# Attention plus gated mixer on one core: where the guard's flag is made, where block 1 is transposed, and where three small masks are built

## The chip, the cores and the metric

One Trainium2 chip, one core. The metric is the device time of one launch in microseconds, smaller is better. A core has a matrix engine (PE, with its weight loads as a row of their own, PEld), VectorE (DVE), ScalarE (ACT), GpSimd (POOL) and the sync engine (SP), which mostly issues DMAs. Each engine works through its own instructions in program order and waits on semaphores that others raise.

## The reference

```python
xn = layernorm(x)                               # 2048 tokens, 512 wide
out = x + A(xn, wqkv, wo) + B(xn, w_in, w_sp, b_sp, w_out)

A:  q, k, v = split(xn @ wqkv)                  # 32 heads of 16
    scores = q @ k.T * 16 ** -0.5, masked to 0 <= i - j < 256
    return softmax(scores) @ v @ wo
B:  z = gelu(xn @ w_in)                         # 1376 wide, halves of 688
    z1, z2 = z[:, :688], layernorm(z[:, 688:])
    g = w_sp @ z2 + b_sp[:, None]               # w_sp: 2048 x 2048
    return (z1 * g) @ w_out
```

## The kernel before

The tokens lie in 16 blocks of 128. The kernel has three stages, and in each the program order of every engine is written out by hand.

**Start.** The loads of x and w_in are issued on SP's and ScalarE's queues. Ten matmuls on zeros (`heat`) run meanwhile, and VectorE and POOL build constants: the identity, and the band masks `maskY` and `maskD`. From `maskD` VectorE builds `maskC` with three small instructions (L235, L238, L242); it is first read by `do_mask` in the second stage. Then, for blocks 0 to 3: statistics of x (`ln_sums` L249, `ln_single`: L253 and L267), the reciprocal root as a power on POOL (L270), and `ln_apply` (L290), which writes `xn`. `transposes` turns the four 128x128 chunks of `xn` on PE (L306) and ScalarE copies the result to `xnT` (L309); from block 4 on this is a DMA instead (L299). Block 0 is turned in two parts.

**Stage 1.** For each block z = gelu(xn @ w_in): `z_mm` (L317) adds up four chunks c of the 512 inputs, in two halves of 688 and in two pieces j of 344 for each. For block 0 the first two chunks of both halves are done first (eight matmuls), then block 1 is transposed, then `z_rest(0)` adds chunks 2 and 3 of the first half, and `z_split(1)` does block 1's first half in two separate banks (`zo`); `z_rest(1)` comes behind. Between the z of later blocks come the projections to q, k and v (`qkv_unit`). PE runs in program order, so an instruction that waits holds up all behind it.

**Stage 2.** A text `ORDER` lists the steps: S scores and their exponentials, m masks, p products with v, n normalization, g the token mixing, f the output. `f_work(t, c0)` makes one output block `fo` in a PSUM bank (two banks, tag f, shared with o and gf): 6 matmuls with w_out (L539), 4 with wo (L546); then VectorE adds x to it (L553), which frees the bank, and a DMA writes it out (L557). At the start of each `f_work` the x of block t + 2 is loaded on SP (`load_xo`, L524; four buffers). Block 15 is done in two halves of 256 columns, written out by SP and by ScalarE. ORDER ends with `p p f n n 10 f10 f10 f10 f10`: two products, the start of block 12, the last two normalizations, block 12, 13, 14, and the two halves of 15.

**The guard.** The softmax is computed without subtracting a maximum. `check_sums` tests all reciprocals of the sums (`r_all`) against two limits (L719, L720, which also counts), and moves the 128 counts to one row by a small DMA on SP (L725). `make_flag` takes the row's minimum (L730) and compares it (L733), and `read_flag` loads the flag into a register of every engine (L739). `tc.If` (L928) then runs a safe version of the whole where the flag is set; here it is not, and every engine branches past it. `check_sums` is called at the end of the last `normalize`, `make_flag` ahead of the add of block 15's first half, and `read_flag` ahead of the add of its second. Behind the branch come some semaphore steps and a barrier of all engines (shown as L953), where SP also waits for the last DMAs.

Of the kernel before, what the change touches and what calls it, by code (L numbers as in the profile page):

```python
# [8 lines left out]
P = 128  # L9
# [3 lines left out]
ALU = mybir.AluOpType  # L13
# [9 lines left out]
HALF = 344  # L23
NB = S_TOK // P
NC = D // P
NG = 4
NJ = NB // 2
# [7 lines left out]
PAD = 64  # L35
# [17 lines left out]
def kernel(  # L53
# [12 lines left out]
    nc = tc.nc  # L66
# [16 lines left out]
    maskD = pers.tile([P, P], BF, name="maskD")  # L83
    maskC = pers.tile([P, 2, PAD], BF, name="maskC")
# [8 lines left out]
    flag = pers.tile([P, 1], mybir.dt.int32, name="flag")  # L93
# [48 lines left out]
    with ExitStack() as actx:  # L142
# [50 lines left out]
        for _ in range(WARM):  # L193
# [9 lines left out]
            out=hmask[:],  # L203
            in_=ident[:].rearrange("p (s e d) -> p e s d", s=4, e=2),
# [3 lines left out]
        for m, off, old, new in ((maskY, 0, PAD, 0), (maskD, -PAD, 0, PAD)):  # L208
            nc.gpsimd.memset(m[:], 1.0)
            nc.gpsimd.affine_select(  # L210
                out=m[:, old : old + PAD], in_=m[:, old : old + PAD], pattern=[[-1, PAD]],
# [3 lines left out]
                out=m[:, new : new + PAD], in_=m[:, new : new + PAD], pattern=[[1, PAD]],  # L215
# [12 lines left out]
        def write_ones():  # L228
# [3 lines left out]
                in_=one[p0:p1, :].unsqueeze(1).to_broadcast([p1 - p0, m1 - m0, H]),  # L232
            )

        nc.vector.tensor_tensor(  # L235
            out=maskC[:, 0, :], in0=maskD[:, 0:PAD], in1=maskD[:, PAD:P], op=ALU.add
        )
        nc.vector.tensor_scalar(  # L238
            out=maskC[:, 1, :], in0=maskC[:, 0, :], scalar1=-1.0, scalar2=1.0,
            op0=ALU.mult, op1=ALU.add,  # L240
        )
        nc.vector.tensor_copy(out=maskC[0:PAD, 1, :], in_=maskC[0:PAD, 0, :])  # L242

        mvx = {}
        rsx = {}

# [5 lines left out]
        def ln_mean(n, b0, mvt, stats):  # L252
            nc.vector.bn_aggr(out=mvt[:, n - b0, :], in_=stats[:])  # L253
            mvx[n] = mvt[:, n - b0, 0:1]
# [4 lines left out]
        def ln_single(n, stats):  # L259
            mvt = sm.tile([P, 4, 2], F32, name="mvt")  # L260
            ln_mean(n, n, mvt, stats)
            rsx[n] = rstd(mvt, 1)[:, 0:1]

        def rstd(mvt, k):
            ve = sm.tile([P, 4], F32, name="ve")
            rs = sm.tile([P, 4], F32, name="rs")
            nc.vector.tensor_scalar(  # L267
                out=ve[:, 0:k], in0=mvt[:, 0:k, 1], scalar1=LN_EPS, scalar2=None, op0=ALU.add
            )
            nc.gpsimd.tensor_tensor(  # L270
                out=rs[:, 0:k], in0=ve[:, 0:k], in1=mhalf[:, 0:k], op=ALU.pow
            )
            return rs
# [11 lines left out]
        def ln_apply(n, parts=1):  # L285
            xs = xts[n // 4][:, n % 4, :]
            xn = lt.tile([P, D], BF, name="xn")
            w = D // parts
            for i in range(parts):
                nc.vector.tensor_scalar(  # L290
                    out=xn[:, i * w : (i + 1) * w], in0=xs[:, i * w : (i + 1) * w],
                    scalar1=mvx[n], scalar2=rsx[n], op0=ALU.subtract, op1=ALU.mult,
                )
            return xn

        def transposes(n, xn, parts=1):
            t0 = PAD + n * P
            if n >= 4:
                nc.sync.dma_start_transpose(out=xnT[:, :, t0 : t0 + P], in_=xn[:])  # L299
                return  # L300
            w = NC // parts
            for i in range(parts):
                tp = psum["f"].tile([P, w, P], BF, name="tp", tag="f")
                for c in range(w):
                    k = i * w + c
                    nc.tensor.transpose(  # L306
                        out=tp[:, c, :], in_=xn[:, k * P : (k + 1) * P], identity=ident[:]
                    )
                nc.scalar.copy(out=xnT[:, i * w : (i + 1) * w, t0 : t0 + P], in_=tp[:])  # L309

        def z_tile():
            return ps_s.tile([P, 2, 512], F32, name="zp", tag="S")

        def z_mm(n, half, j, out, chunks):
            f0 = half * FH + j * HALF
            for c in chunks:
                nc.tensor.matmul(  # L317
                    out, lhsT=xnT[:, c, PAD + n * P : PAD + (n + 1) * P],
                    rhs=w_in_sb[:, c, f0 : f0 + HALF],
                    start=(c == 0), stop=(c == NC - 1),  # L320
                )
# [45 lines left out]
        xns = {}  # L367
        ln_single(0, ln_sums(0))
        sums1 = ln_sums(1)
        xns[0] = ln_apply(0, 2)  # L370
        ln_single(1, sums1)
        xns[1] = ln_apply(1)
        ln_single(2, ln_sums(2))
        sums3 = ln_sums(3)
# [2 lines left out]
        xns[3] = ln_apply(3)  # L377
        transposes(0, xns.pop(0), 2)
        zps = [z_tile(), z_tile()]
        for c in range(2):  # L380
            for half in range(2):
                for j in range(2):
                    z_mm(0, half, j, zps[half][:, j, 0:HALF], [c])
        transposes(1, xns.pop(1))

        def z_rest(half):
            for c in range(2, NC):
# [7 lines left out]
        for n in range(NB):  # L395
            b, j = divmod(n, 4)
# [132 lines left out]
    def f_cols(t):  # L529
        return D // 2 if t == NB - 1 else D  # L530

    def f_work(t, c0):
        if c0 == 0 and t + 2 < NB:
            load_xo(t + 2)
        xo = xos[t]
        w = f_cols(t)
        fo = ps_x.tile([P, 512], F32, name="fo", tag="f")
        for ch in range(NFC):
            nc.tensor.matmul(  # L539
                fo[:, 0:w], lhsT=uTs[t][:, ch, :], rhs=w_out_sb[:, ch, c0 : c0 + w],  # L540
                start=(ch == 0), stop=False,
            )
            yield
        q0 = t % 2 * P
        for c in range(NC):
            nc.tensor.matmul(  # L546
                fo[:, 0:w], lhsT=oTs[t // 2][:, c, q0 : q0 + P], rhs=wo_sb[:, c, c0 : c0 + w],
                start=False, stop=(c == NC - 1),
            )
            yield  # L550
        if t == NB - 1:
            (read_flag if c0 else make_flag)()
        nc.vector.tensor_tensor(  # L553
            out=xo[:, c0 : c0 + w], in0=fo[:, 0:w], in1=xo[:, c0 : c0 + w], op=ALU.add
        )
        eng = nc.scalar if c0 else nc.sync
        eng.dma_start(out=out2[t * P : (t + 1) * P, c0 : c0 + w], in_=xo[:, c0 : c0 + w])  # L557

    E = {}
    ED = {}  # L560
    turned = {}
    later = []
# [39 lines left out]
    def normalize(J, G):  # L602
        ot = turned.pop((J, G))
        rsum = r_all[:, J * NG + G, :]
        nc.vector.reciprocal(out=rsum, in_=ot[:, :, DH])
        on = late().tile([P, 8, 32], BF, name="on", bufs=2)
        nc.vector.tensor_tensor(
            out=on[:].rearrange("p b (e d) -> p e b d", e=2),
            in0=ot[:].rearrange("p (e b) j -> p e b j", e=2)[:, :, :, 0:DH],
            in1=rsum.rearrange("p (e b) -> p e b", e=2).unsqueeze(3).to_broadcast([P, 2, 8, DH]),  # L610
            op=ALU.mult,
        )
        if G == 0:
            oTs[J] = late().tile([P, NC, 256], BF, name="oT", bufs=3)
        nc.vector.transpose(
            out=oTs[J][:, G, :], in_=on[:].rearrange("p b j -> p (b j)")
        )
        if (J, G) == (NJ - 1, NG - 1):
            check_sums()

    groups = [(0, 0, "P"), (0, 1, "P"), (0, 0, "Q"), (0, 0, "D")]
    groups += [(0, 2, "P"), (0, 3, "P"), (0, 2, "Q")]
# [86 lines left out]
        mul(cells(G)[:, 8:16, 0:4:2, :], both[:, 0:1, :].to_broadcast([P, 2, PAD]))  # L709

    rows = []
    again = []

    def check_sums():
        assert not (later or units)
        r = r_all[:].rearrange("p a b -> p (a b)")
        ok = ep.tile([P, 512], BF, name="ok", tag="E")
        low = ep.tile([P, 1], F32, name="low", tag="E")
        nc.vector.tensor_scalar(out=ok[:], in0=r, scalar1=R_LOW, scalar2=None, op0=ALU.is_ge)  # L719
        nc.vector.scalar_tensor_tensor(  # L720
            out=ok[:], in0=r, scalar=R_HIGH, in1=ok[:], op0=ALU.is_le, op1=ALU.mult,
            accum_out=low[:],
        )
        row = ep.tile([P, P], F32, name="row", tag="E")
        nc.sync.dma_start(out=row[0:1, :], in_=low[:])  # L725
        rows.append(row)

    def make_flag():
        low = sm.tile([P, 1], F32, name="low")
        nc.vector.tensor_reduce(  # L730
            out=low[0:1, :], in_=rows[0][0:1, :], axis=mybir.AxisListType.X, op=ALU.min
        )
        nc.vector.tensor_scalar(  # L733
            out=flag[0:1, :], in0=low[0:1, :], scalar1=16.0 * NJ * NG, scalar2=None, op0=ALU.is_lt
        )

    def read_flag():
        again.append(
            nc.values_load(  # L739
                flag[0:1, 0:1], min_val=0, max_val=1,  # L740
                skip_runtime_bounds_check_because="a comparison gives 0 or 1",
            )
        )


# [154 lines left out]
    units = [(J, G) for J in range(NJ) for G in range(NG)]  # L900
# [6 lines left out]
    for step in ORDER.split():  # L907
# [8 lines left out]
        else:  # L916
# [7 lines left out]
            if left == 0:  # L924
                assert next(unit, None) is None
    assert not (left or groups or masks or units or later or any(work.values()))
    late_ctx.close()
    with tc.If(again[0] > 0):  # L928
        with ExitStack() as gctx:
            attention_with_maximum(gctx)  # L930

# [26 lines left out]
```

## Time and profile before

| | us |
|---|---|
| median of 3 runs | 258.0 (257.42 to 259.27) |
| profiled execution, time | 257.84 |
| profiled execution, span | 256.0 |
| PE busy | 249.4 (97%) |
| VectorE busy | 203.6 (80%) |
| ScalarE busy | 194.0 (76%) |
| POOL busy | 20.6 (8%) |

Granted PE clock: 1.000. The span runs from the first to the last instruction; the profiled execution's time is 1.8 us longer.

Busy time by stretch (us from the start of the span, number of instructions in brackets):

```profile
0.00:4.00 4.00, 2.73 (x7) 1.04 (x8) 2.70 (x14) 0.03 (x1) 1.85 (x12) 1.00 0.49 169
4.00:8.00 4.00, 3.07 (x22) 1.53 (x20) 2.80 (x10) 2.11 (x4) 1.12 (x2) 1.00 1.05 366
8.00:13.00 5.00, 4.91 (x40) 3.24 (x38) 4.07 (x14) 4.33 (x8) 1.10 (x2) 1.00 1.01 364
13.00:83.00 70.00, 70.00 (x400) 38.56 (x397) 52.46 (x152) 42.42 (x68) 9.95 (x15) 1.00 0.37 72
83.00:242.00 159.00, 159.00 (x3149) 90.36 (x3150) 134.00 (x222) 145.10 (x156) 6.53 (x19) 1.00 0.52 103
242.00:247.00 5.00, 4.88 (x76) 2.59 (x69) 4.81 (x12) 0.00 (x0) 0.00 (x0) 1.00 0.22 43
247.00:252.00 5.00, 4.77 (x32) 2.83 (x29) 2.51 (x7) 0.00 (x0) 0.00 (x0) 1.00 0.47 131
252.00:256.00 4.00, 0.00 (x0) 0.00 (x0) 0.29 (x1) 0.00 (x0) 0.00 (x0) 1.00 0.17 43
```

The columns are the stretch, its length, the busy time of PE, PEld, VectorE, ScalarE and POOL, PE's clock, the DMA engines' busy share and GB/s. Waits are put down to what came last; lines as "L317" are lines of the kernel, and a q behind an engine's name (SPq) is its sequencer or queue.

### The profile page before, as it was taken

What the parts mean: (1) busy time and instruction counts of PE and PEld (TensorE: products, weight loads), DVE (VectorE), ACT (ScalarE), POOL (GpSimd) and SP (SyncE); (2) the same over time, 40 slices, a digit from 0 to 9 for tenths busy, and PEclk for the clock granted to TensorE, in tenths of its full rate; (3) what the DMA queues carried; (4) which work ended last, traced back from release to release, by engine and by line L of the source; (5) the groups of instructions that cost most, each with busy time, mean ns of one, the idle gap of its engine ahead of it and who ended that gap; (6) DMA issues with size and microseconds to landing.
All of it is one profiled execution on the core that took longest, in us unless ns stands there. A gap on an engine that the chain in (4) does not pass through costs nothing.

```text
span 256.0 us, 8488 instructions
## 1 busy us (share of the span) xinstructions
PE 249.4 (97%) x3700; PEld 140.2 (55%) x3700; DVE 203.6 (80%) x426; ACT 194.0 (76%) x234; POOL 20.6 (8%) x50
## 2 busy tenths in 40 slices
PE   6999999999999999999999999999999999999993
PEld 2655555555555465565455655556456554556642
DVE  7798976974747787988887978688797899788872
ACT  2776468466456999989889989988989999999100
POOL 3232111111011240000000000000000000000000
PEclk9999999999999999999999999999999999999999
DMA  6969341028200236883547082729616568270223
GB/s 244 361 150 255 62 63 22 1 60 120 67 1 0 60 50 138 115 141 81 142 35 188 26 197 57 159 62 160 157 43 97 117 108 166 79 130 28 41 68 89
DMA packets 65689, 26.50 MB, mean 103 GB/s; under 512 B 55872, under 2 KB 63856, under 8 KB 65648
## 3 DMA queue, kind: packets, MB, share of 16 engines
q1 hardware_dynamic: 64784, 24.89, 46.5%
q10 hardware_dynamic: 864, 1.03, 1.2%
q8 instruction: 30, 0.49, 0.9%
q14 instruction: 11, 0.09, 0.1%
HBM read 8.41 MB, written 2.10 MB: 41 GB/s over the span
## 4 chain that ended last, share of the span: by engine, by line
PE 94%; DVE 3%; DMA 1%; issue 0%; ACT 0%; POOL 0%; DVEq 0%
PE gf L503 31%; PE zp L317 14%; PE S L634 10%; PE o L592 9%; PE fo L539 8%; PE pj_o L110 6%; PE fo L546 5%; PE pj_f L110 4%; PE pj_f L128 3%; PE pj_o L128 2%; DMA xt<-in_A_x_dram 1%; DVE ot L599 1%; PE zo L317 1%; DVE xo L553 0%; PE tp L306 0%
## 5 line engine op out<-in xcount | busy, mean ns | idle before, releaser
L684 ACT ACTIVATE E<-S 128x1024 bf16<-128x1024 f32 x124 | 116.9, 1045 | 8.9 <-PE S L634 8.7
L503 PE MATMUL gf<-z2n,wspT 128*128 128x344 bf16 x512 | 83.0, 310 | 0.0
L503 PEld LDWEIGHTS <-wspT 128*128 128x128 bf16 x512 | 46.5, 98 | 29.3 <-issue 7.9
L317 PE MATMUL zp<-w_in_sb,xnT 128*128 128x344 bf16 x248 | 40.9, 309 | 0.2 <-ACT xnT L309 0.2
L690 DVE TENSOR_TENSOR E<-E,maskY 128x2048 bf16<-128x2048 bf16 (+1 forms) x34 | 37.6, 1115 | 3.1 <-ACT E L684 3.1
L317 PEld LDWEIGHTS <-xnT 128*128 128x128 bf16 x256 | 24.8, 98 | 16.0 <-ACT xnT L309 0.8
L634 PE MATMUL S<-qpad,kT 32*128 32x256 bf16 (+2 forms) x848 | 31.7, 260 | 0.0
L662 ACT ACTIVATE ED<-S 128x1024 bf16<-128x1024 f32 x30 | 29.3, 1041 | 0.5 <-PE S L634 0.5
L599 DVE STREAM_TRANSPOSE ot<-o 128x512 f32<-128x512 f32 x32 | 22.2, 715 | 7.4 <-PE o L592 7.4
L509 DVE SCALAR_TENSOR_TENSOR u<-gf,b_all,z 128x344 bf16<-128x344 f32 x32 | 18.3, 572 | 8.5 <-PE gf L503 8.1
L539 PE MATMUL fo<-w_out_sb,uT 128*128 128x512 bf16 (+1 forms) x102 | 24.6, 367 | 0.2
L634 PEld LDWEIGHTS <-kT 32*128 32x128 bf16 (+1 forms) x848 | 11.1, 98 | 21.6 <-issue 20.7
L592 PE MATMUL o<-E,v_y 128*32 128x128 bf16 (+1 forms) x736 | 22.8, 239 | 0.0
L121 DVE TENSOR_SCALAR qpad<-qt,hmask 128x512 bf16<-128x512 bf16 x32 | 9.8, 348 | 14.3 <-ACT qt L119 14.3
L592 PE MATMUL o<-ED,vh 128*32 128x64 bf16 x960 | 21.0, 193 | 0.0
L325 ACT ACTIVATE z2n<-zp 128x688 bf16<-128x688 f32 x16 | 11.9, 744 | 10.8 <-PE zp L317 10.7
L110 PE MATMUL pj_o<-xnT,wqkv 128*128 128x512 bf16 x76 | 19.5, 379 | 0.0
L110 PEld LDWEIGHTS <-wqkv 128*128 128x128 bf16 x128 | 12.5, 98 | 12.6
L325 ACT ACTIVATE z<-zp 128x688 bf16<-128x688 f32 x15 | 11.2, 744 | 10.8 <-PE zp L317 10.8
L690 DVE TENSOR_TENSOR ED<-ED,maskC 128x2048 bf16<-128x2048 bf16 x15 | 18.1, 1204 | 0.0
L270 POOL TENSOR_TENSOR rs<-ve,mhalf 128x2 f32<-128x2 f32 (+1 forms) x18 | 12.0, 667 | 67.9 <-DVE ve L267 67.9
L592 PEld LDWEIGHTS <-vh 128*32 128x32 bf16 x960 | 17.2, 98 | 0.1
(73 smaller groups left out, 240.6 us busy)
## 6 DMA issues: line engine op xcount, KB each, us to landing
vh<-v_y SPq DMA_DIRECT2D x16, 140.0 KB, 3.1
xo<-in_A_x_dram SPq DMA_DIRECT2D x16, 128.0 KB, 2.5
out_dram<-xo SPq DMA_DIRECT2D x15, 128.0 KB, 2.4
xt<-in_A_x_dram SPq DMA_DIRECT2D x3, 512.0 KB, 5.3
wqkv<-in_A_wqkv_dram SPq DMA_DIRECT2D x1, 1536.0 KB, 8.7
w_out_sb<-in_B_w_out_dram SPq DMA_DIRECT2D x1, 640.0 KB, 6.0
wo_sb<-in_A_wo_dram SPq DMA_DIRECT2D x1, 512.0 KB, 4.0
w_in_sb<-in_B_w_in_dram ACTq DMA_DIRECT2D x1, 344.0 KB, 4.2
```

Source lines behind the costliest of these rows:

```text
L110: nc.tensor.matmul(pt[:], lhsT=wqkv[:, c, w0 : w0 + P], rhs=xnT[:, c, t0 : t0 + 512], start=(c == 0), stop=(c == NC - 1),)
L317: nc.tensor.matmul(out, lhsT=xnT[:, c, PAD + n * P : PAD + (n + 1) * P], rhs=w_in_sb[:, c, f0 : f0 + HALF], start=(c == 0), stop=(c == NC ...
L325: nc.scalar.activation(out=dst.rearrange("p (j f) -> p j f", j=2), in_=zp[:, :, 0:HALF], func=ACT.Gelu_apprx_tanh,)
L503: nc.tensor.matmul(gf[:, 0:HALF], lhsT=wspT[t][:, c, :], rhs=z2n[:, c, j * HALF : (j + 1) * HALF], start=(c == 0), stop=(c == NB - 1),)
L509: nc.vector.scalar_tensor_tensor(out=u[:, j * HALF : (j + 1) * HALF], in0=gf[:, 0:HALF], scalar=b_all[:, t : t + 1], in1=z1[:, t, j * HALF ...
L539: nc.tensor.matmul(fo[:, 0:w], lhsT=uTs[t][:, ch, :], rhs=w_out_sb[:, ch, c0 : c0 + w], start=(ch == 0), stop=False,)
L592: nc.tensor.matmul(o[32 * s : 32 * s + 32, c0 + r0 : c0 + r0 + n], lhsT=v[:, m, h * VW : h * VW + 32], rhs=rhs(s), start=(i == 0), stop=(i ...
L599: nc.vector.transpose(out=ot[:].rearrange("p b j -> p (b j)"), in_=o[:])
L634: nc.tensor.matmul(out, lhsT=kT[32 * s : 32 * s + 32, g, k0 : k0 + nk], rhs=qpad[J // 2][32 * s : 32 * s + 32, g, :, qs - q00 : qs - q00 + ...
L662: nc.scalar.activation(out=Ed[:, 16 * i : 16 * i + 16, :], in_=S[i][:].rearrange("p b (x q) -> p (b x) q", q=PAD), func=ACT.Exp, scale=SM_ ...
L684: nc.scalar.activation(out=E[(J, G)][:, b0 + 2 * i : b0 + 2 * i + 2, :], in_=S[i][:], func=ACT.Exp, scale=SM_SCALE,)
L690: nc.vector.tensor_tensor(out=v, in0=v, in1=mask.unsqueeze(1).to_broadcast([P, v.shape[1], *mask.shape[1:]]), op=ALU.mult,)
```

## The change

Three parts. The three instructions that build `maskC` move from the constants to behind `ln_single(1, ...)`, ahead of block 1's apply. Block 1's transposes move ahead of the last two of block 0's first eight z matmuls. `check_sums` is called at the end of the first `f_work` that ends with no product and no normalization left (block 12), behind its add and output; `make_flag` and `read_flag` are called behind everything else, right ahead of `tc.If`.

```diff
-        nc.vector.tensor_tensor(
-            out=maskC[:, 0, :], in0=maskD[:, 0:PAD], in1=maskD[:, PAD:P], op=ALU.add
-        )
-        nc.vector.tensor_scalar(
-            out=maskC[:, 1, :], in0=maskC[:, 0, :], scalar1=-1.0, scalar2=1.0,
-            op0=ALU.mult, op1=ALU.add,
-        )
-        nc.vector.tensor_copy(out=maskC[0:PAD, 1, :], in_=maskC[0:PAD, 0, :])
...
         xns[0] = ln_apply(0, 2)
         ln_single(1, sums1)
+        nc.vector.tensor_tensor(
+            out=maskC[:, 0, :], in0=maskD[:, 0:PAD], in1=maskD[:, PAD:P], op=ALU.add
+        )
+        nc.vector.tensor_scalar(
+            out=maskC[:, 1, :], in0=maskC[:, 0, :], scalar1=-1.0, scalar2=1.0,
+            op0=ALU.mult, op1=ALU.add,
+        )
+        nc.vector.tensor_copy(out=maskC[0:PAD, 1, :], in_=maskC[0:PAD, 0, :])
         xns[1] = ln_apply(1)
...
         zps = [z_tile(), z_tile()]
-        for c in range(2):
-            for half in range(2):
-                for j in range(2):
-                    z_mm(0, half, j, zps[half][:, j, 0:HALF], [c])
-        transposes(1, xns.pop(1))
+        for c, half in ((0, 0), (0, 1), (1, 0), (1, 1)):
+            if (c, half) == (1, 1):
+                transposes(1, xns.pop(1))
+            for j in range(2):
+                z_mm(0, half, j, zps[half][:, j, 0:HALF], [c])
...
-        if t == NB - 1:
-            (read_flag if c0 else make_flag)()
         nc.vector.tensor_tensor(
             out=xo[:, c0 : c0 + w], in0=fo[:, 0:w], in1=xo[:, c0 : c0 + w], op=ALU.add
         )
         eng = nc.scalar if c0 else nc.sync
         eng.dma_start(out=out2[t * P : (t + 1) * P, c0 : c0 + w], in_=xo[:, c0 : c0 + w])
+        if not (rows or units or later):
+            check_sums()
...
-        if (J, G) == (NJ - 1, NG - 1):
-            check_sums()
...
     def read_flag():
-        again.append(
-            nc.values_load(
-                flag[0:1, 0:1], min_val=0, max_val=1,
-                skip_runtime_bounds_check_because="a comparison gives 0 or 1",
-            )
+        return nc.values_load(
+            flag[0:1, 0:1], min_val=0, max_val=1,
+            skip_runtime_bounds_check_because="a comparison gives 0 or 1",
         )
...
+    make_flag()
     late_ctx.close()
-    with tc.If(again[0] > 0):
+    with tc.If(read_flag() > 0):
         with ExitStack() as gctx:
             attention_with_maximum(gctx)
```

More of the change, by code (lines that the diff above doesn't have):

```diff
@@ L711 @@
     rows = []
-    again = []
     def check_sums():
```

## The prediction

> **What bounds the kernel now.** I read the page, then the chain of waits in order of time for the first 14 us and from 240 us on, then the timelines there, the rows of single lines, and the DMA rows of the last 4 us. The page gives PE 97% busy and 94% of the chain, at clock 1.00. In the table by stretches PE is busy for all of 13 to 242 us, so a saving can only lie in the first 13 us, in the last 14, or in being carried unchanged through the middle. The end, in the chain of waits:
>
> ```profile
> 245.16 0.45 DVE oT L615
> 245.60 0.32 DVE ok L719
> ...
> 246.65 0.61 DVE xo L553
> ...
> 247.30 1.45 PE fo L539 x6
> ...
> 251.87 0.42 DVE xo L553
> ```
>
> Columns: start, us, what. VectorE's two range checks (L719, L720) stand ahead of the add of block 12 (L553), which frees the PSUM bank for block 14. After 252.29 the page's chain has nothing, though the span runs to 256.0 (256.03 in the trace). The DMA rows of 251.0 to 255.4 us, 40 slices of 0.11 us, show what fills it:
>
> ```profile
> DMA  0004998200000593000069202104100100000000
> GB/s 28 0 0 149 317 372 280 75 0 0 0 0 0 172 433 98 5 0 0 23 195 312 65 0 79 19 9 93 9 9 5 14 19 5 0 0 0 0 0 0
> q8 instruction: 1, 0.02, 1.8%
> q14 instruction: 3, 0.02, 1.7%
> out_dram<-xo SPq DMA_DIRECT2D x1, 64.0 KB, 3.4
> out_dram<-xo ACTq DMA_DIRECT2D x1, 64.0 KB, 2.8
> ```
>
> Block 15's two output halves (issued 251.61 and 252.32) move nearly all their bytes by 252.8 and 253.4, then a trickle goes on to 254.7; they land at 251.61 + 3.4 = 255.0 and 252.32 + 2.8 = 255.1. The same stretch holds four instruction fetches; in the trace's packets they run one after another, 252.64 to 253.94, then 253.37 to 254.40, and the last output packets follow them. So one DMA engine serves the fetches, and the last sixteenth of both halves queues behind. The fetches follow the guard's branches:
>
> ```profile
> L928 PEldq COMPARE_BRANCH x1: 358/358/358, 251.5 to 251.5; - x1
> L928 SPq COMPARE_BRANCH x1: 58/58/58, 252.6 to 252.6; - x1
> L928 SPq EVENT_SEMAPHORE x3: 17/17/17, 253.1 to 253.3; - x3
> L953 SPq EVENT_SEMAPHORE x10: 17/28/28, 253.4 to 256.0; - x10
> ```
>
> PE branches at 251.50 and the first fetch packet starts 1.14 later. SP's closing waits are done by 253.73 but for those on the two landings, the last met at 255.17; 0.87 of barrier follows, to 256.03.
>
> The start, in the timeline:
>
> ```profile
> 6.35 0.56 POOL L270 TENSOR_TENSOR rs<-ve,mhalf 128x1 f32<-128x1 f32 x1 [0.99 <-DVE ve L267]
> 6.54 1.34 PE L317 MATMUL zp<-w_in_sb,xnT 128*128 128x344 bf16 x8 [0.21 <-ACT xnT L309]
> 6.95 0.41 DVE L290 TENSOR_SCALAR xn<-xt,mvt,rs 128x512 bf16<-128x512 bf16 x1 [0.68 <-POOL rs L270]
> 7.72 0.39 PE L306 MATMUL tp<-ident,xn 128*128 128x128 bf16 x4
> 8.14 0.59 ACT L309 COPY xnT<-tp 128x512 bf16<-128x512 bf16 x1 [1.38 <-PE tp L306]
> 8.78 1.34 PE L317 MATMUL zo<-w_in_sb,xnT 128*128 128x344 bf16 x8
> ```
>
> PE issues a z matmul every 0.146 us; block 0's last one starts at 8.38, so zo could start at 8.53. It starts at 8.78, after the copy of block 1's transpose: a hole of 0.26.
>
> **Block 1's transposes ahead of two z matmuls.** They start two matmuls, 0.29 us, earlier: 7.43. Their input (apply at 6.95, 0.41 long, then 0.056 as from the first apply to its transpose) is there at 7.42, 0.01 early. The copy then ends at 8.43, ScalarE being idle, and zo starts at 8.53: minus 0.26. Next late is nothing: block 0's Gelu starts at 8.73 as now (it waits for the matmul ending at 8.69); the loads of w_in's remaining chunks land at 7.99 and 8.81 and are wanted at 9.7; block 2's apply ends at 9.88 and is wanted at 10.3, block 3's at 11.23, wanted at 11.7; wqkv lands at 14.7, wanted at 15.6. Those covers shrink by 0.26 and hold. The middle carries the 0.26, PE having no other wait there; it is worth 0 if one appears, and 0.26 cannot be exceeded. I take 0.26, since every wait that is listed for PE itself lies before 8.8 us.
>
> **The masks.** Three VectorE instructions leave 2.96 to 3.58. That gains nothing: the first statistics start at 3.61, when ScalarE's queue passes a wait on the same load of x, also at 3.61. The load ends there. In the new place VectorE idles 0.68 before the apply at 6.95, waiting for POOL. The rows before give steps of 0.23 and 0.22 between the masks and 0.17 for the third, 0.62 in all; from 6.2 to 6.3 they end at 6.8 to 6.9. Cost 0; without that cover 0.6 on block 1's apply. They now run beside POOL's power (6.35). Powers last 0.55 to 0.74 us; the longest, 0.73 and 0.74, have VectorE's TENSOR_SCALAR beside them, others with it 0.69. So 0 to 0.05, and I take 0.
> [...]
>
> **The end: range check behind block 12's add.** L719 and L720 (0.42 and 0.62 from start to start) leave the place ahead of that add, which moves from 246.56 to about 245.53. PE gets block 14's bank early, but is itself busy until 247.10 (block 13 began at 244.94; six and four matmuls of 0.216). So fo of block 14 starts at 247.10, not 247.30: minus 0.20. On SP the row's DMA, with 3.6 us of waiting, stood ahead of the load of xo 14 (issued 247.38, landed 249.7, with 1.8 us of VectorE idle for it). Now the load stands ahead and can go at 243.1, behind the uT transpose; the output that its buffer held before was issued at 218.6. The add of block 14 follows PE at 249.5 instead of 249.82. The row goes behind block 12's output, at about 247.4 for 0.53; xo 15's load follows at 248.05 instead of 248.54 and, with 2.54 as now, lands at 250.6. Block 15's halves then follow PE: adds near 250.7 and 251.66 (now 251.16 and 251.87). ScalarE issues the last output at 252.12.
>
> **The end: flag and branch last.** The flag is now made behind the last add. Steps as in the trace: reduce 0.34 behind the start of a 0.43 us add (it starts 0.08 before the add of block 14 ends), 252.00; flag 0.30 later, 252.30; loads on all five engines 0.17 later, 252.47; SP's load 0.53 and 0.08, branch at 253.08; 0.53 to the next instruction, 253.61; 0.70 of semaphores, 254.31; 0.87 of barrier, 255.18. Queued behind the loads is only the branch and the barrier, but all engines wait for them. Cover: by the 1.14 above, fetches start near 254.2, when the last output, moved 1.1 to 1.55 us after its issue, has landed at 253.7. So a landing at 255.1 is exchanged for a flag chain that ends at 254.3; the end goes from 256.03 to 255.18, minus 0.85, the 0.20 in it. Bounds: loads took 0.47 to 0.58 and branch to next instruction 0.17 (POOL) to 0.61 (VectorE), so plus or minus 0.2.
>
> **Sum.** 256.03 - 0.26 - 0.85 = 254.92; the profiled execution took 257.84, 1.81 outside its span: 256.73. The median of the three runs is 0.16 higher: 256.9.
>
> **Rivals.** *The fetches still meet the output* (they follow the stream's pages, not the branch). Then the late sixteenth stays, and only 0.20 and 0.26 are won: 257.5. For it: fetches run all through the page, one per 16 KB. Against: three q14 fetches within 0.7 us right after five branches, and few before.
> *The branch waits for its code*, slower. All five engines now branch together at 253.08 with nothing left to hide them. If the target's code has to come first, fetches of 1.14 + 1.77 (252.64 to 254.40) end at 255.99 rather than the 253.61 above: 2.38 later, 1.27 over before after both gains: 259.3. It decides from a stall of 1.11 on. Against: SP's next instruction came 0.53 after its branch, PE's 0.42, both ahead of any fetch packet. For: something was fetched then, and the closing barrier was always later than it.
> [...]
> [...]
> *It does not do what it says*: another late transfer holds the end and nothing moves, 258.0.
>
> **Chances.** Forecast 0.52 (its own range 256.3 to 257.4), output still met 0.17, masks hold up the power 0.10, code stall 0.14, nothing 0.07. The runs before lie from 0.6 under to 1.3 over their median. The low end is the forecast less 0.2 for the flag chain and the 0.6 of a median's own error, with a little over: 256.0; the high end takes in "nothing" and small stalls: 258.3. It leaves out the larger stalls. One per cent, 2.6 us, is about what a measurement can tell from no change; none of the cases reaches it but by scatter: faster 0.03, within 0.94, slower 0.03.
>
> **What would show it.** zo at 8.5 with no hole behind block 0's z; the apply of block 1 still at 6.95 (later: masks); the first range check behind block 12's add; fo of block 14 at once behind block 13; the load of xo 14 at 243; flag near 252.0 and branches near 252.8, in the shifted time; both last outputs landed within 1.7 us; fetches only behind them; next instruction 0.5 behind the branch. A gap of over 1 us there would make the prediction wrong, as would PE waits in the middle.

## The result and the profile after

The changed kernel takes 256.64 us (median of 8 runs, 256.39 to 257.23) against 257.77 (8 runs, 257.42 to 259.27): ratio 0.9953, 95% interval 0.9938 to 0.9968, or 1.13 us less. Its profiled execution took 256.39 us with a span of 254.7 (254.68 in the trace); forecast were 256.9 and 254.92. Run again beside the last experiments it took 256.60 against 257.83 (0.9948, 0.9936 to 0.9961).

The chain of waits at the end of the changed kernel (start, us, what):

```profile
246.85 1.29 PE fo L538 x6
...
251.23 0.42 DVE xo L550
251.65 0.19 DVE low L726
...
251.87 0.14 DVE flag L729
```

The range checks are gone from it. Block 14 (246.85) follows block 13 without a gap, PE runs on to the last add, and the guard's minimum and flag hang behind that add. The rows of the branch show the rest (duration, then first and last start):

```profile
L923 SPq EVENT_SEMAPHORE  x3: 17/17/17, 253.1 to 253.3; - x3
L923 SPq COMPARE_BRANCH  x1: 58/58/58, 252.6 to 252.6; - x1
```

All five engines branch between 252.6 and 252.7, and SP's next instruction comes 0.53 us later, as before the change. The DMA rows of 249.8 to 254.2 us, in slices of 0.11 us:

```profile
DMA  0000000499820018820000000694000000058000
...
q14 instruction: 3, 0.02, 2.2%
q8 instruction: 1, 0.02, 1.4%
...
out_dram<-xo SPq DMA_DIRECT2D x1, 64.0 KB, 1.5
out_dram<-xo ACTq DMA_DIRECT2D x1, 64.0 KB, 1.6
```

The two output halves are the groups around 251.6 and 252.7 and land 1.5 and 1.6 us after their issue, where it was 3.4 and 2.8; no trickle follows them. The last group is the code fetches, from 253.67 on, behind everything. SP meets the last landing in passing and is through its waits at 253.84.

The start, in the timeline of the changed kernel:

```profile
5.93 0.18 DVE L363 TENSOR_TENSOR maskC<-maskD 128x64 bf16<-128x64 bf16 x1
...
6.09 0.56 POOL L261 TENSOR_TENSOR rs<-ve,mhalf 128x1 f32<-128x1 f32 x1 [1.00 <-DVE ve L258]
6.15 0.18 DVE L366 TENSOR_SCALAR maskC<-maskC 128x64 bf16<-128x64 bf16 x1
...
6.37 0.17 DVE L370 COPY maskC<-maskC 64x64 bf16<-64x64 bf16 x1
...
6.70 0.41 DVE L281 TENSOR_SCALAR xn<-xt,mvt,rs 128x512 bf16<-128x512 bf16 x1 [0.16 <-POOL rs L261]
...
7.28 0.39 PE L297 MATMUL tp<-ident,xn 128*128 128x128 bf16 x4
...
8.38 1.33 PE L308 MATMUL zo<-w_in_sb,xnT 128*128 128x344 bf16 x8
```

Block 1's transposes stand two matmuls earlier, and zo starts at 8.38 with no hole ahead of it. Of the masks, the second and the third lie inside the power, and neither they nor the power are longer for it; the first ends only 0.02 us behind the power's start. Block 1's apply starts 0.60 us behind the power's start, as before the change.

### The profile page after: what moved, and what is told of

It is laid out like the page before. It is cut to its first block, busy times and chain, and to the rows that moved or that the text cites. A ratio compares the mean times of both kernels' runs of the same rounds, so it can differ in the third digit from the quotient of the medians.

```text
span 254.7 us, 8488 instructions
## 1 busy us (share of the span) xinstructions
PE 249.6 (98%) x3700; PEld 140.3 (55%) x3700; DVE 203.5 (80%) x426; ACT 193.8 (76%) x234; POOL 20.5 (8%) x50
## 4 chain that ended last, share of the span: by engine, by line
PE 98%; DVE 1%; ACT 0%; issue 0%
PE gf L502 31%; PE zp L308 14%; PE S L631 10%; PE fo L538 9%; PE o L591 9%; PE pj_o L110 6%; PE fo L545 6%; PE pj_f L110 4%; PE pj_f L128 3%; PE pj_o L128 2%; PE heat L194 2%; PE zo L308 0%; PE tp L297 0%; DVE ot L598 0%; DVE xo L550 0%; ACT xnT L300 0%
```

## The experiments

Before: 257.82 us (27 runs, or 11 in the second group), 257.83 (17 runs) for the last four.

| what was run | median us | ratio to before, 95% interval | span of its profile |
|---|---|---|---|
| transposes alone | 257.64 | 0.9992, 0.9983 to 1.0001 | 256.0 |
| masks alone | 258.00 | 1.0005, 0.9996 to 1.0015 | 256.5 |
| guard alone | 256.85 | 0.9964, 0.9950 to 0.9977 | 255.0 |
| range check moved alone | 257.48 | 0.9990, 0.9981 to 0.9999 | 256.0 |
| flag and load moved alone | 257.10 | 0.9971, 0.9960 to 0.9982 | 255.4 |
| no branch | 255.94 | 0.9924, 0.9910 to 0.9938 | 254.2 |
| minimum first | 256.17 | 0.9934, 0.9921 to 0.9948 | 254.6 |
| nine zero matmuls | 256.48 | 0.9949, 0.9936 to 0.9963 | 256.7 |
| changed kernel again | 256.60 | 0.9948, 0.9936 to 0.9961 | 255.1 |
| masks unmoved | 256.60 | 0.9955, 0.9938 to 0.9972 | 254.7 |
| minimum first again | 256.29 | 0.9934, 0.9921 to 0.9948 | 254.5 |
| flag before the add | 257.95 | 1.0001, 0.9992 to 1.0009 | 255.9 |

**Transposes alone.** On the kernel before:

```diff
+            if (c, half) == (1, 1):
+                transposes(1, xns.pop(1))
...
-        transposes(1, xns.pop(1))
```

> Only block 1's transposes are moved. If the hole ahead of zo was the wait for block 1's copy and the middle carries a saving, zo starts straight behind block 0's last z matmul, the span falls by 0.26 us to 255.8 and the time to about 0.999 of before. If some later wait takes it back, zo starts early and the span stays at 256.0. If block 1's xn is not there in time, PE waits ahead of the transposes and zo stays near 8.8.

zo starts at 8.48, straight behind the matmul ahead of it, and the last gf matmul at 240.58 instead of 240.83: the middle carries the 0.25. The span stays at 256.0 all the same, as the second case of the expectation has it, but the wait that takes the gain back stands at the very end: the last output, though issued 0.24 earlier, lands at 255.12, nearly as before (255.15). The four fetches came 0.23 earlier too, but took 2.80 us in all instead of 2.50. The median falls by 0.18, with an interval that just reaches no change.

**Masks alone.** Only the three instructions move.

```diff
         ln_single(1, sums1)
+        nc.vector.tensor_tensor(
+            out=maskC[:, 0, :], in0=maskD[:, 0:PAD], in1=maskD[:, PAD:P], op=ALU.add
+        )
...
         xns[1] = ln_apply(1)
```

> Only the three mask instructions are moved. Theory of the prediction: the first statistics wait for the load of x, so nothing is won. Rival, from the changed kernel's trace, where the statistics began at 3.36 us: the load often lands before the masks would be done (3.58), and up to 0.25 us is won at the start, of which PE, busy with the zero matmuls until 5.7 us, keeps 0.1 to 0.15: span 255.9. If masks and POOL's power exclude each other, block 1's apply starts 0.4 us late and the power is 0.2 to 0.6 us longer than 0.56.

No gain. The masks run at 6.13 to 6.73 beside the power (6.29, 0.56 long), and block 1's apply is at 6.89, 0.60 behind the power's start, as before. The second and the third mask (0.18 us from 6.35, 0.17 from 6.56) and the power did not exclude each other; the first ends as the power begins (6.31 against 6.29) and does not tell. The span of 256.5 is not the masks' doing: the first z matmuls of this execution came 0.26 to 0.29 us apart instead of 0.146, and zo only at 9.16 (more under the last heading).

**Guard alone.**

```diff
-        if t == NB - 1:
-            (read_flag if c0 else make_flag)()
...
+        if not (rows or units or later):
+            check_sums()
...
+    make_flag()
     late_ctx.close()
+    read_flag()
```

> Only the guard is moved, all three of its steps. If the last output's late landing was from the code fetches behind the branches, both halves of block 15 land within 1.7 us, the branches come near 253.1, the fetches near 254.2 and the span is 255.2 (0.85 less). If the fetches follow the instruction stream and not the branch, one half still lands 2.5 us or more behind its issue and the span is 255.8.

The halves land 1.5 and 1.6 us behind their issue, SP branches at 252.88, the first fetch starts at 253.98, the span is 254.97. 0.97 us of the median is here. This kernel is the changed one without the moves of transposes and masks: its median, 256.85, lies 0.2 above the changed kernel's 256.64 and 256.60.

**Range check moved alone.** As above, without the flag's part.

```diff
         eng.dma_start(out=out2[t * P : (t + 1) * P, c0 : c0 + w], in_=xo[:, c0 : c0 + w])
+        if not (rows or units or later):
+            check_sums()
```

> Only the range check and its row DMA go behind block 12's add; flag and its load stay ahead of block 15's adds. Then block 14's matmuls start 0.2 us earlier, but the branches come at 251 to 252 us and the fetches still meet the last outputs: a landing of 2.5 us or more, span 255.6 to 255.9. If the order of the check were what counts, the span would be the 255.2 of the whole guard change.

Block 14 starts at 247.09 (247.30 before) and the last add at 251.64 (251.87). The branches lie between 251.1 and 252.5 and the second half lands 3.0 us behind its issue. So the order of the check frees 0.2 us on PE, and in this execution the late landing takes all of it back: 0.0 off the span. The median of 11 runs is 0.34 lower, but they lie from 257.31 to 258.00 and the profiled one took 257.83; what the order alone is worth stays open.

**Flag and load moved alone.** The check stays ahead of block 12's add.

```diff
-        if t == NB - 1:
-            (read_flag if c0 else make_flag)()
...
+    make_flag()
     late_ctx.close()
+    read_flag()
```

> Only the flag and its load go behind the last add; the range check stays ahead of block 12's add. If the fetches follow the branch, the late landing goes, but block 14 starts 0.2 us later than with the check moved as well: span 255.4. If the fetches follow the instruction stream, the landing stays late and the span is near 256.0.

The span is 255.4; branches at 253.4, fetches from 254.44, landings after 1.5 and 1.6 us. The median is 0.72 lower than before.

**No branch.** On the changed kernel; the safe version for sums out of range is left out of the computation.

```diff
-    with tc.If(read_flag() > 0):
-        with ExitStack() as gctx:
-            attention_with_maximum(gctx)
```

> The changed kernel without the load of the flag, the branch and the safe version behind it (left out of the computation; the flag is still made). If branches cause the fetches, no group of four instruction fetches stands at the end, and the end is the landing of the last output: near 251.7 + 1.6 + 0.9 = 254.2 us, 0.45 less than the changed kernel. If fetches come with the stream anyway, they are there at 252 to 254 and a landing is late: span 254.7 or more.

The DMA rows of 251.0 to 254.2 us, in slices of 0.08:

```profile
DMA  9610000698300000000004995000000000000000
...
q1 hardware_dynamic: 209, 0.12, 11.9%
q10 hardware_dynamic: 144, 0.07, 7.2%
```

There is no instruction queue in it: without the branch no code is fetched here, and the last output lands 1.6 us after its issue. The span of 254.2 is what that landing and the barrier cost. From the start of the last add to the end it is 2.87 us here and 3.45 in the changed kernel, so the guard's chain costs 0.58 (0.66 between the medians 255.94 and 256.60). This run takes away the branch and the safe version's code together, so by itself it does not tell which of them brings the fetches; the runs that move only the branch do.

**Minimum first.** On the changed kernel; run twice, the second time beside the changed kernel.

```diff
+        if t == NB - 1 and c0:
+            lows.append(reduce_row())
         nc.vector.tensor_tensor(
             out=xo[:, c0 : c0 + w], in0=fo[:, 0:w], in1=xo[:, c0 : c0 + w], op=ALU.add
```

> The changed kernel with the row's minimum taken ahead of the last add, in VectorE's idle time there, so that only the comparison stands behind the add. If the chain of flag, load, branch and barrier sets the end, it gets 0.30 us shorter: span 254.4, branches near 252.3, fetches near 253.4, just behind the last output's packets (253.1). If the fetches then meet those packets, the last output lands later than 1.7 us and nothing or less is won.

> The kernel with the row's minimum ahead of the last add, beside the changed kernel on one chip: 0.30 us less than that by the length of the chain from the last add to SP's branch (1.06 us in its profile, 1.36 in the changed kernel's). If its lower median was the chip's or the start's, they are the same here.

From the last add to SP's branch it is 1.05 and 1.06 us, where the changed kernel had 1.36 both times, and the last output still lands after 1.6. On the same chip the median is 256.29 (255.93 to 256.55) against 256.60 (256.53 to 256.81): the 0.30 expected, and a kernel faster than the changed one. The intervals of the two ratios to before overlap, but five of its six runs lie below all six of the changed kernel.

**Flag before the add.** The same idea one step further; the load and the branch stay last.

```diff
+        if t == NB - 1 and c0:
+            make_flag()
         nc.vector.tensor_tensor(
             out=xo[:, c0 : c0 + w], in0=fo[:, 0:w], in1=xo[:, c0 : c0 + w], op=ALU.add
...
-    make_flag()
```

> The changed kernel with minimum and comparison both ahead of the last add; load and branch stay last. If the branch's code fetches, 1.1 us behind it, are what delays the last output, the branches now come near 251.8, the fetches near 252.9, on the last output's packets (252.9 to 253.2), and a part of it lands 2.3 us or more behind its issue: span near 255.3, slower than the changed kernel by 0.3 to 0.8. If an earlier flag simply shortens the chain, the span is 254.2, the end that the last output sets.

The DMA rows of 251.0 to 255.4 us, slices of 0.11:

```profile
DMA  9300069400000002950300000301000000000000
...
q14 instruction: 3, 0.02, 2.3%
q8 instruction: 1, 0.02, 1.6%
...
out_dram<-xo ACTq DMA_DIRECT2D x1, 64.0 KB, 3.2
```

PE's branch, in the rows of the branch:

```profile
L924 PEldq COMPARE_BRANCH  x1: 358/358/358, 251.7 to 251.7; - x1
```

The flag is there at 250.91 instead of 251.87. POOL, PE and SP branch at 251.65 to 251.72, fetches start at 252.82, and the last output's group (at 252.8) has the trickle behind it again. It lands 3.2 us after its issue, the span is 255.9 and the median is that of the kernel before, 257.95, and so 1.35 above the changed kernel: more than the 0.3 to 0.8 expected. An earlier flag made the kernel slower by the fetches that it let loose.

**Masks unmoved.** The changed kernel with `maskC` built among the constants.

> The changed kernel with the masks left among the constants. In the profiles with the masks there the first statistics began at 3.50 us at the earliest, without them at 3.36. If that is what the masks are worth, this kernel is at most 0.14 us slower than the changed one, and its first statistics begin at 3.50 or later; by the prediction it is the same.

> The changed kernel once more, beside the next three on one chip. Its parts alone took 0.18 (transposes), -0.18 (masks) and 0.97 us (guard) off the median; if they add up, it is 1.0 to 1.2 us under the kernel before. If the zero matmuls at the start leave PE at half rate in some execution, that one is 0.3 to 2 us longer, and z matmuls come 0.29 us apart at its start.

Both have a median of 256.60. With the masks unmoved the first statistics began at 3.50, just behind the load's landing at 3.47; in the changed kernel run again they began at 3.44. The masks' move is worth nothing that 6 runs can show. The parts alone sum to 0.97 us (0.18 - 0.18 + 0.97), and the whole gave 1.13 and 1.23, the second just above the 1.0 to 1.2 expected. The interval of the first, 0.82 to 1.60, holds the sum, that of the second, 1.01 to 1.65, just not; the parts have intervals of their own of 0.4 us and more in width, so no gain beyond the sum is shown. None of the six executions of the changed kernel was 0.3 us longer than the others.

The changed kernel run again has a span of 255.1 in its profile, where the first had 254.7. Most of that is a wait of PE in the middle, 0.36 us long and over at 101.5 us:

```profile
PE gf L502 <- DMA wspT<-in_B_w_sp_dram: 0.4, 1, 0.4
```

A load of w_sp landed late there. The kernel without the branch shows the same wait with 0.2 us, the other twelve profiles none.

**Nine zero matmuls.** On the changed kernel.

```diff
-WARM = 10
+WARM = 9
```

> The changed kernel with 9 zero matmuls at the start instead of 10. In the changed kernel's chain these run until 5.71 us and the first transposes, ready at 5.5, stand behind them. If they bind, the first copy of block 0 comes 0.1 to 0.15 us earlier and the span is 254.55. If the load of x is what the start waits for, no change; if nine warm PE too little, the granted clock at the start falls and z matmuls come slower than every 0.146 us.

The profiled execution took 258.4 us, five others 256.36 to 256.70. Its chain, at the start:

```profile
6.47 1.90 PE zp L308 x6
8.37 0.43 PE tp L297 x4
8.80 1.72 PE zp L308 x6
```

Six z matmuls take 1.7 to 1.9 us where the changed kernel's took 0.9 to 1.05, and four transposes 0.43 where it was 0.22. PE's matmuls came at half rate until 10.4, and zo came at 10.31. Whether the five others gained the 0.1 stays open; one of six lost 1.9. That nine zero matmuls caused it is not shown: with ten, the profile of the masks alone began late as well.

## Why the prediction was right

**The end.** The claim that the span's last microseconds were a landing held up by code fetches, and the fetches a consequence of the branches, is shown from three sides: without the branch there are no fetches and the landing takes 1.6 us; with all branches behind the output it takes 1.6 us and the fetches come later; with the flag about 1 us earlier, and load and branch still last, it takes 3.2 us again. The end of the span follows: from the start of the last add to the end it is 3.45 to 3.46 us in all six profiles where the whole flag, the load and the branch stand behind that add, 3.14 in both with the minimum first, 2.87 without the branch, and 4.2 to 4.5 in the five where fetches meet the output.

The 16 KB fetch (q8) followed PE's branch by 1.14 us before the change, by 1.14 in the changed kernel and by 1.13 in the one with the early flag. Nine of the thirteen profiles with a branch have 1.12 to 1.16; the other four have 1.26, 1.34, 1.59 and 1.72. The three 8 KB fetches (q14) in turn fit the branches of SP, ScalarE and VectorE: in the changed kernel and in the one with the early flag each starts 1.07 to 1.19 us behind one of them. So the rival by which these fetches follow the instruction stream (30 of 16 KB on q8 in the span before) and not the branch falls.

One step of the mechanism was too simple: that one DMA engine serves the fetches. Before the change the q8 fetch (252.64 to 253.94) and the first q14 fetch (from 253.37) overlap, and the late packets come in three groups of eight, a sixteenth of 128 each: one of the first half, starting at 253.92 as the q8 fetch ends, and two of the second, one starting at 253.74 as the first q14 fetch ends and one behind the first half's group. With the early flag two sixteenths are late in the same way (253.38 and 253.95, behind fetches that end at 253.38 and 253.96). That fits two engines of the sixteen; the trace does not name them. The forecast does not hang on it.

**Its size.** The chain was put together from single rows: last add to SP's branch 1.42 us (measured 1.36), to the next instruction 0.53 (0.53), semaphores 0.70 (0.69), barrier 0.87 (0.87). Block 14 followed block 13 at once; xo 14's load went at 242.72 and xo 15's at 247.61, forecast 242.84 and 247.79 when the 0.26 of the start is taken off.

**The transposes.** Forecast 0.26, carried through the middle. Alone they moved the last gf matmul by 0.25. What was not seen is that with the old end they would be worth less than that in the profile: a saving that the end's fetches swallowed. In the whole change the end no longer depends on the fetches, and the 0.2 between the medians of the guard alone and of the changed kernel is about what transposes and masks are worth there. The prediction named the condition for it, no other wait of PE in the middle. It held in twelve of fourteen profiles, the changed kernel's first one among them; in the two others PE waited for w_sp.

**The masks.** Forecast 0, and no difference measured. The reason given holds in the main: statistics wait for the load, and start within 0.04 us of its landing in every profile. That the load ends at 3.61 was one execution's value; in the thirteen other profiles the statistics began between 3.36 and 3.64. With the masks among the constants they began at 3.50 at the earliest, 0.09 behind the start of the third mask, so for a load as early as the changed kernel's (3.34) the masks would have been in the way by up to 0.14 us. The medians show none of it. This is the term that was off: the changed kernel's profile had the early load, zo came at 8.38 rather than 8.53, and of the 0.24 us by which its span lies under the forecast 0.15 is this and 0.06 the shorter chain at the end. The early load is scatter of a start; what the masks' move let through of it is not shown. PE's half rate took a part back (last heading): its zero matmuls ran until 5.71.

**The rivals on the slow side.** *The branch waits for its code* did not come: in the changed kernel all engines went on 0.41 to 0.61 us after the branch but POOL (0.17), at least 0.38 us ahead of the first fetch packet. That a branch has to wait for its code was not shown: no stall is seen. What the runs add is that the fetches behind this branch can hold up data: the last output landed 2.8 us after its issue before the change and 3.2 with the early flag, where it is 1.6 in the changed kernel. Masks that hold up the power, a chance of 0.10, did not come either: a TENSOR_SCALAR of 0.18 and a copy of 0.17 us lay inside the power's 0.56, each as long as before, so these two (128x64 and 64x64) and the power (128x1) did not run in turn. The first mask overlaps the power by 0.02 us only, so for it nothing is shown, and the runs do not say what larger operands would do.

## What to carry to other kernels

When a span goes on for microseconds behind the last computation, look at the landing of the last output against the usual landing of its size, and at what else the DMA engines carry in that stretch; here the 16 KB code fetch came 1.1 to 1.7 us behind PE's branch, and an output in flight then landed 1.2 to 2.0 us late for one or two of its sixteen parts. So the place of a guard's branch near the end is a choice with two sides: as early as its fetches meet the last output it cost 1.35 us, and simply last it left 0.30 us to be won. Put it where its fetches come just behind the last packets, and shorten what stands between. A branch so early that its fetches are done before the last output was not tried. A saving earlier in the program counts only if the end moves with it.

## What the runs showed that was not expected

PE begins at half rate: the zero matmuls start every 0.427 us at first, and before the change the last two are 0.216 apart. The moment from which the matmuls came closer varied from profile to profile: at about 4.0 us with the masks unmoved, between 4.2 and 4.5 before the change, after 5.9 in the changed kernel, at 7.3 in the one with the masks alone and at 10.4 in the one with nine zero matmuls. The page's row of granted clock shows 9 in every slice of all of them; only the distance between matmuls tells. From the first statistics to zo it is 5.61 us with the masks alone, where the four other profiles with block 1's transposes unmoved have 5.17 to 5.22, and 6.88 with nine zero matmuls, where the eight others with the transposes moved have 4.90 to 5.03. So the longer half rate cost about 0.4 and 1.9 us, the second more than the whole change won. The moments lie 2.7 to 9.1 us behind the first zero matmul (at 1.27), and the runs do not show why. Whether more zero matmuls would guard against it was not tried.
